# Column maxima over 128 partitions: from TensorE's transposes to a reduction on GpSimd

## The chip, the cores and the metric

The kernel runs on one core of one Trainium2 chip. A core has five engines with an instruction queue each: TensorE (PE in the profile; PEld is its weight load), VectorE (DVE), ScalarE (ACT), GpSimd (POOL) and SyncE (SP). All but SP compute on SBUF, a memory of 128 partitions; PE writes to PSUM, which DVE and ACT read and GpSimd does not. An engine works through its queue in order and waits on semaphores for the others. The metric is the device time of one execution in microseconds. Before the change it is 846.99 us, the median of three runs (846.04 to 847.17).

## The reference

Eight batches of linear attention, and one gated feed-forward layer over all their tokens:

```python
q_s = exp(q - max(q, axis=-1));  q_s = q_s / (sum(q_s, axis=-1) + 1e-9)
k_s = exp(k - max(k, axis=2));   k_s = k_s / (sum(k_s, axis=2) + 1e-9)   # axis 2: the sequence
kv  = einsum('bhsd,bhse->bhde', k_s, v)
x   = einsum('bhsd,bhde->bhse', q_s, kv)       # -> 4608 tokens x 512
h   = x @ w_in                                 # 512 -> 2048
out = (h * erf(softplus(h))) @ w_out           # 2048 -> 512
```

q, k and v have shape 8 x 8 heads x 576 x 64, all in float32. The maximum of k runs over the sequence. The sequence lies on the partitions, so this maximum goes across them: it needs the largest of 128 partitions for each of 512 columns (8 heads of 64), and then every partition needs the result.

## The kernel before

**Feed-forward.** The 4608 tokens are taken in 12 blocks of 384 (three to a pair of batches), and each block in four groups of 512 hidden columns: 48 steps n. In a step, `mm1` multiplies weights with x (banks pX, pY, pZ), `softplus` and `erf` run on ACT, `gmul`, `ghi` and `glo` (L1037, L1051, L1055) multiply and split the result into two float16 tiles on DVE, and `mm2` (L1083) adds three float16 products for each float32 one into banks o0 to o2. The products of `mm1` (L957) are a seven-product scheme, whose sums are made as the banks pX, pY, pZ are emptied: by DVE at L969, L971, L979 and L982, by ACT at L974, L976 and L984. Each of these three banks exists once, so the next product into it waits until it is empty. The first six steps are in float32 (`mm1_32`, L1074), while the weights are being decoded.

**Attention.** Batch 0 is written out at the start. `attention(b)` for batches 1 to 7 is a generator: it is traced in pieces between the steps of the feed-forward, `pace` taking pieces as fast as the shares in `SHARES` say. For each batch it does the following.

- `k_max` (L503 to L507, DVE): maxima of k within each partition, into `asc[:, 0]`, 128 x 512. `asc` is one tile with two halves of 512 columns; the second half is a scratch of the same function, and later other steps use both.
- `k_max_T` (L514, L518): four PE transposes put the 512 columns onto partitions, in a PSUM bank with the tag `bk`; DVE reduces them to `km`, 128 x 4.
- `q_sub` (L460, L461, DVE): the maxima of q along the row, and their subtraction.
- `k_max_rows` (L527): four PE transposes of the broadcast `km` put the maximum of each column onto all partitions, in the other `bk` bank, `kB`.
- L683, L688 (DVE): k and its tail less `kB`. Then the exponentials on ACT, the products k'v on PE (`kv_mm`, L548), and their normalisation (`kv_norm`, L567 to L571) into `asc[:, 0]`.
- `kv_max`, `kv_split`: DVE takes the largest magnitude of each partition (L584, `mx`, 128 x 1); `all_max` makes it one number for all partitions by a PE transpose of the broadcast column (L128) and a DVE reduction (L130, `e`); from it `scale_of_max` derives a power of two and its inverse (L131 to L144), and L601 and L602 split the scaled k'v into two float16 tiles `kvbd`.
- `x_mm` (L660): q times kvbd on PE; ACT writes the result into the block x (L449).

**What GpSimd does.** Constants and zero fills at the start, one subtraction for batch 0 (L826), some weight loads (L191), the zero fill of `kvbd` for batches 2 and 3 (L596), and for each batch two small fills of `vtail` (L439, L440) ahead of the load of v's last rows.

**What sets the order.** `ORDER` and the loops at the end give the program order by hand. A planner then makes each engine's queue from it when the program is built: program order is its priority, and its own estimate of durations tells it when an instruction is ready; an instruction that is ready early may run in a gap ahead of older ones. On ACT the feed-forward's functions and the exponentials are chained to program order (`act`). Semaphores and waits follow from the tiles.

## Time and profile before

| | |
|---|---|
| median of three runs | 846.99 us (846.04 to 847.17) |
| profiled execution: time, span | 847.39 us, 845.4 us |
| granted TensorE clock | 1.0 of full speed |
| PE busy | 817.5 us, 97% |
| DVE busy | 631.9 us, 75% |
| ACT busy | 506.6 us, 60% |
| POOL busy | 18.1 us, 2%, 37 instructions |
| kT transposes (L514), kB transposes (L527), the scale's (L128) | 32, 32 and 8 matmuls of 128x128 in float32 |

The profile is one execution; its times count from the first instruction. A line of the timeline is: start, length, engine, line, operation, tile written <- tiles read, shapes, count, and in brackets the idle time before it and what ended that. PE's matmuls overlap and their ends are modelled, so the cost of one in PE's stream is the distance to the next start, not its length.

### The profile page before, as it was taken

What the parts mean: (1) busy time and instruction counts of PE and PEld (TensorE: products, weight loads), DVE (VectorE), ACT (ScalarE), POOL (GpSimd) and SP (SyncE); (2) the same over time, 40 slices, a digit from 0 to 9 for tenths busy, and PEclk for the clock granted to TensorE, in tenths of its full rate; (3) what the DMA queues carried; (4) which work ended last, traced back from release to release, by engine and by line L of the source; (5) the groups of instructions that cost most, each with busy time, mean ns of one, the idle gap of its engine ahead of it and who ended that gap; (6) DMA issues with size and microseconds to landing.
All of it is one profiled execution on the core that took longest, in us unless ns stands there. A gap on an engine that the chain in (4) does not pass through costs nothing.

```text
span 845.4 us, 15123 instructions
## 1 busy us (share of the span) xinstructions
PE 817.5 (97%) x6336; PEld 554.3 (66%) x6336; DVE 631.9 (75%) x900; ACT 506.6 (60%) x638; POOL 18.1 (2%) x37
## 2 busy tenths in 40 slices
PE   3999999999999999999999999999999999999996
PEld 2655555666766766766776776766776776767662
DVE  6899689998998869867877769867876657553543
ACT  2597659876674567465665467465665475544532
POOL 2101100000000000000000000000000000000000
PEclk9999999999999999999999999999999999999999
DMA  9975920023226303411171203411131100100100
GB/s 267 403 189 168 210 52 38 1 58 75 63 51 127 88 19 76 106 38 27 46 151 30 76 19 76 106 39 26 40 74 13 40 1 1 39 1 2 38 1 38
DMA packets 141347, 61.53 MB, mean 73 GB/s; under 512 B 130528, under 2 KB 132576, under 8 KB 141280
## 3 DMA queue, kind: packets, MB, share of 16 engines
q1 hardware_dynamic: 139104, 52.18, 24.9%
q0 software_dynamic: 2176, 8.39, 2.9%
q8 instruction: 50, 0.82, 0.4%
q14 instruction: 17, 0.14, 0.1%
HBM read 45.09 MB, written 9.44 MB: 64 GB/s over the span
## 4 chain that ended last, share of the span: by engine, by line
PE 66%; DVE 16%; ACT 10%; DMA 3%; issue 3%; SPq 1%; POOL 0%; ACTq 0%; DVEq 0%; POOLq 0%
PE o L1083 28%; PE pX L957 15%; PE pZ L957 8%; PE o L1074 4%; ACT G L350 3%; PE pY L957 3%; ACT L350 3%; DVE G L1037 2%; PE kv L548 2%; DVE H L1055 2%; DMA q<-in_q_dram 1%; PE x L660 1%; SPq L415 1%; ACT wt L301 1%; DVE wt L302 1%
## 5 line engine op out<-in xcount | busy, mean ns | idle before, releaser
L1083 PE MATMUL o<-wt,H 128*128 128x512 f16 x1512 | 347.4, 379 | 1.8 <-DVE H L1051 1.3
L957 PEld LDWEIGHTS <-wt 128*128 128x128 f16 x3528 | 294.0, 98 | 29.3 <-issue 5.6
L1083 PEld LDWEIGHTS <-H 128*128 128x128 f16 x1512 | 145.9, 98 | 150.8 <-DVE H L1051 1.8
L957 PE MATMUL pX<-x,wt 128*128 128x192 f16 x2016 | 193.9, 246 | 1.8 <-ACT H L976 0.7
L350 ACT ACT_TABLE_LOAD x105 | 134.7, 1283 | 3.2 <-DVE H L982 1.2
L1037 DVE SCALAR_TENSOR_TENSOR G<-G,small,H 128x1536 f32<-128x1536 f32 x44 | 79.9, 1817 | 46.2 <-ACT G L350 45.9
L984 ACT COPY H<-pX 128x384 f32<-128x384 f32 x42 | 20.0, 477 | 136.8 <-PE pX L957 131.4
L957 PE MATMUL pZ<-x,wt 128*128 128x192 f16 x1008 | 98.2, 246 | 0.0
L350 ACT ACTIVATE G<-H,U 128x768 f32<-128x768 f32 (+1 forms) x56 | 69.3, 1255 | 22.1 <-DVE H L982 21.5
L1055 DVE TENSOR_TENSOR H<-G,H 128x1536 f16<-128x1536 f32 x42 | 73.8, 1756 | 1.0
L350 ACT ACTIVATE G<-G 128x1536 f32<-128x1536 f32 x48 | 71.3, 1486 | 0.5
L449 ACT ACTIVATE x<-x 128x384 f32<-128x384 f32 (+1 forms) x52 | 17.7, 388 | 59.4 <-PE x L660 56.9
L957 PE MATMUL pY<-x,wt 128*128 128x192 f16 x504 | 48.4, 246 | 0.0
L982 DVE TENSOR_TENSOR H<-pZ,H 128x384 f32<-128x384 f32 x42 | 23.2, 553 | 28.9 <-PE pZ L957 28.9
L301 ACT ACTIVATE x<-x 128x768 f16<-128x768 f32 (+1 forms) x44 | 32.9, 762 | 16.4 <-DVE x L394 16.3
L969 DVE COPY H<-pY 128x384 f32<-128x384 f32 x42 | 23.3, 554 | 25.8 <-PE pY L957 25.8
L1051 DVE CAST H<-G 128x1536 f16<-128x1536 f32 x42 | 40.2, 957 | 0.8
L302 DVE SCALAR_TENSOR_TENSOR x<-x,x 128x768 f16<-128x768 f32 (+1 forms) x44 | 37.4, 853 | 3.2 <-ACT x L301 3.2
L1099 DVE TENSOR_SCALAR ob<-o,V 128x512 f32<-128x512 f32 x29 | 21.7, 749 | 21.9 <-PE o L1083 21.8
L996 PE MATMUL pX<-x,wt 128*128 128x384 f32 x96 | 33.9, 488 | 0.0
L971 DVE TENSOR_TENSOR H<-pX,H 128x384 f32<-128x384 f32 x42 | 23.3, 555 | 13.3 <-PE pX L957 12.5
L460 DVE TENSOR_REDUCE q_m<-q 128x16 f32<-128x1024 f32 x14 | 17.1, 1219 | 17.9 <-DMA q<-in_q_dram 17.9
(182 smaller groups left out, 851.1 us busy)
## 6 DMA issues: line engine op xcount, KB each, us to landing
out_dram<-ob SPq DMA_DIRECT2D x32, 256.0 KB, 2.3
vbuf<-in_v_dram SPq DMA_DIRECT2D x60, 128.0 KB, 3.2
q<-in_q_dram SPq DMA_DIRECT2D x56, 128.0 KB, 3.3
k<-in_k_dram SPq DMA_DIRECT2D x56, 128.0 KB, 3.4
wt<-in_moe_w_out_dram POOLq DMA_DIRECT2D x5, 1024.0 KB, 8.7
wt<-in_moe_w_in_dram SPq DMA_DIRECT2D x4, 1024.0 KB, 10.6
wt<-in_moe_w_out_dram SPq DMA_DIRECT2D x2, 1024.0 KB, 15.6
H_raw<-in_k_dram SPq DMA_DIRECT2D x2, 512.0 KB, 5.0
```

Source lines behind the costliest of these rows:

```text
L301: nc.scalar.activation(hi, src, AF.Copy, scale=s)
L302: nc.vector.scalar_tensor_tensor(lo, src, s, hi, op0=ALU.mult, op1=ALU.subtract)
L350: i = nc.scalar.activation(out_, in_, func, **kw)
L957: nc.tensor.matmul(o, w[wl][:, c, a * P:(a + 1) * P], x[:, xl, xi, c, :], start=(new and a == 0 and c == 0 and i == 0), stop=(c == 1 and i ...
L969: nc.vector.tensor_copy(C[0, 0], bank2("Y"))
L971: add(C[0, 0], bank2("X"), C[0, 0], op=ALU.add)
L996: nc.tensor.matmul(ph[:, :T], w[:, c, a * P:(a + 1) * P], x[:, c, :], start=(c == 0), stop=(c == NC4 - 1),)
L1037: nc.vector.scalar_tensor_tensor(flat(s["G"]), flat(s["G"]), GA32 if n < N32 else GA[:, g:g + 1], flat(s["H"]), op0=ALU.mult, op1=ALU.mult,)
L1051: nc.vector.tensor_copy(flat(s["gh"]), flat(s["G"]))
L1055: nc.vector.tensor_tensor(flat(s["gl"]), flat(s["G"]), flat(s["gh"]), op=ALU.subtract)
L1074: nc.tensor.matmul(o, s["G"][:, a, ts_], w[:, a, :], start=(first_ and a == 0), stop=(last_ and a == FG - 1),)
L1083: nc.tensor.matmul(o, s[gt][:, a, ts_], w[wl][:, a, :], start=(first_ and a == 0 and i == 0), stop=(last_ and a == FG - 1 and i == 2),)
```

## The change

From batch 2 on, two reductions across partitions are one GpSimd instruction each, `partition_all_reduce`, which writes the largest value over 128 partitions to all of them. The first takes `asc[:, 0]` (128 x 512) and writes `asc[:, 1]`, which L683 and L688 then read in the place of the PSUM bank kB. The second takes `mx` (128 x 1) and writes `e`. Batches 0 and 1 keep the transposes, and so do the weights' scales.

```diff
-    def all_max(mx, name):
-
-        bk = psa.tile([P, 512], F32, tag="bk", name=f"{name}_bk")
-        nc.tensor.transpose(bk[:, :P], mx.to_broadcast([P, P]), ident)
+    def all_max(mx, name, pool):
+
         e = at.tile([P, 1], F32, tag="sc_e", name=f"{name}_e")
-        nc.vector.tensor_reduce(e, bk[:, :P], axis=AX.X, op=ALU.max)
+        if pool:
+            nc.gpsimd.partition_all_reduce(e, mx, P, RED.max)
+        else:
+            bk = psa.tile([P, 512], F32, tag="bk", name=f"{name}_bk")
+            nc.tensor.transpose(bk[:, :P], mx.to_broadcast([P, P]), ident)
+            nc.vector.tensor_reduce(e, bk[:, :P], axis=AX.X, op=ALU.max)
         nc.vector.tensor_scalar_max(e, e, TINY)
         return e
...
-    E32, QDMA = 2, 3
+    E32, QDMA, KPOOL = 2, 3, 2
...
-        s, u = scale_of_max(mx, f"x{b}")
+        s, u = scale_of_max(mx, f"x{b}", b >= KPOOL)
...
-        km = k_max_T(b, kmax)
+        if b < KPOOL:
+            km = k_max_T(b, kmax)
+        else:
+            kb = asc[:, 1].rearrange("p (h d) -> p h d", h=H)
+            nc.gpsimd.partition_all_reduce(asc[:, 1], asc[:, 0], P, RED.max)
         q_sub(rows(qs[0]), 16, f"q_{b}_0")
         yield SHARES[1]
-        kb = k_max_rows(b, km)
+        if b < KPOOL:
+            kb = k_max_rows(b, km)
```

## The prediction

> **What bounds the kernel now.** I read the page first: its own span, and who is busy in it.

> ```profile
> span 845.4 us, 15123 instructions
> ...
> PE 817.5 (97%) x6336; PEld 554.3 (66%) x6336; DVE 631.9 (75%) x900; ACT 506.6 (60%) x638; POOL 18.1 (2%) x37
> ```

> Matmul ends are modelled, so 97% alone proves little. I therefore took the busy time by stretches (columns: length, then PE, PEld, DVE, ACT and POOL busy with their counts, clock, DMA share, GB/s), and then the order of PE's own work.

> ```profile
> 150.00:200.00 50.00, 49.59 (x388) 33.31 (x386) 48.03 (x74) 40.41 (x44) 0.63 (x2) 1.00 0.20 46
> 200.00:250.00 50.00, 47.17 (x406) 33.56 (x405) 43.89 (x60) 30.95 (x41) 0.00 (x0) 1.00 0.19 47
> ...
> 350.00:800.00 450.00, 449.48 (x3839) 319.04 (x3838) 310.55 (x428) 256.45 (x302) 1.27 (x4) 1.00 0.18 42
> ```

> From 350 us to 800 us PE lacks 0.52 us in 450, at the full clock (1.00). The timeline shows that this is real work: groups follow one another at a fixed spacing, each starting where the one before ran out.

> ```profile
> 399.35 2.75 PE L1083 MATMUL o<-wt,H 128*128 128x512 f16 x12
> 401.94 0.60 PE L514 MATMUL kT<-ident,asc 128*128 128x128 f32 x4
> 402.38 1.15 PE L957 MATMUL pZ<-x,wt 128*128 128x192 f16 x12
> ...
> 406.34 2.75 PE L1083 MATMUL o<-wt,H 128*128 128x512 f16 x12
> 408.93 0.60 PE L527 MATMUL kB<-ident,km 128*128 128x128 f32 x4
> 409.36 1.15 PE L957 MATMUL pZ<-x,wt 128*128 128x192 f16 x12
> ...
> 439.28 2.75 PE L1083 MATMUL o<-wt,H 128*128 128x512 f16 x12
> 441.87 0.27 PE L128 MATMUL x_bk<-ident,mx 128*128 128x128 f32 x1
> 441.98 1.15 PE L957 MATMUL pZ<-x,wt 128*128 128x192 f16 x12
> ```

> Twelve L1083 matmuls take 2.59 us from start to start, both at 399.35 and at 406.34. So PE's stream is the bound in this stretch, and what leaves the stream is time. Before 350 us it is nearly so, but DVE is close behind: 48.03 of 50 us in the stretch from 150 us. There a late DVE instruction reaches PE at once.

> **Part 1, the transposes that leave PE.** By start-to-start spacing the four kT transposes cost 402.38 − 401.94 = 0.44 us, the four kB 409.36 − 408.93 = 0.43 us, and the scale's one 441.98 − 441.87 = 0.11 us: 0.98 us a batch. Six batches (2 to 7) have the change: 5.9 us.

> One transpose group also stops the stream. In batch 3 PE reaches kB before DVE has the column maxima (km):

> ```profile
> 237.68 0.33 PE L957 MATMUL pZ<-x,wt 128*128 128x192 f16 x2
> 239.22 0.65 PE L527 MATMUL kB<-ident,km 128*128 128x128 f32 x4 [1.21 <-DVE km L518]
> ```

> That wait of 1.21 us goes with kB. What is late next there is DVE's own work, which gets lighter too (below), so I count the 1.2 us in full.

> **Part 2, DVE.** Two groups of its instructions lose their six of eight, and one reads from elsewhere:

> ```profile
> L461 DVE TENSOR_TENSOR q<-q,q_m 128x1024 f32<-128x1024 f32 x14 | 17.1, 1220 | 0.2
> L683 DVE TENSOR_TENSOR k<-k,kB 128x1024 f32<-128x1024 f32 x14 | 16.7, 1216 | 0.3 <-PE kB L527 0.3
> ...
> L518 DVE TENSOR_REDUCE km<-kT 128x4 f32<-128x512 f32 x8 | 5.5, 690 | 7.2 <-PE kT L514 7.2
> ...
> L130 DVE TENSOR_REDUCE x_e<-x_bk 128x1 f32<-128x128 f32 x8 | 2.3, 289 | 5.8 <-PE x_bk L128 5.7
> ```

> DVE loses 0.69 + 0.29 = 0.98 us a batch, as much as PE. So the gain of part 1 also stands where DVE is the closer bound, before 350 us. The subtraction L683 now takes its maxima from SBUF (asc) and not from PSUM (kB). L461 is the same shape with both inputs in SBUF: 1220 against 1216 ns, nothing. No transfer and no ACT instruction is added or moved. Three uses a batch of the two `bk` banks disappear, which can only free them earlier.

> **Part 3, the reductions on GpSimd.** No such instruction is in the trace, so its duration is bounded by other rows of GpSimd:

> ```profile
> 0.24 0.10 POOL L1218 MEMSET const-float32-0.0<- 128x1 f32 x1 [0.24 <-issue]
> ...
> 16.27 1.91 POOL L826 TENSOR_TENSOR q<-G_raw,q_m 128x1024 f32<-128x1024 f32 x1 [12.35 <-DVE q_m L825]
> ...
> 96.17 0.72 POOL L191 DMA_DIRECT2D wt<-in_moe_w_out_dram  x1 [2.47 <-DVE x_s L143]
> ...
> 117.18 0.96 POOL L596 MEMSET kvbd<- 128x1024 f16 x1 [12.58 <-PE x L657]
> 187.09 0.53 POOL L439 MEMSET vtail<- 64x520 f32 x1 [68.94 <-issue]
> ```

> L826 takes 1.91 us for 1024 columns, so 512 columns take at least 0.95 us: the lower end. For the upper end I estimate no overlap at all: eight steps from one group of 16 partitions to the next, and 16 more inside a group, each at L826's rate, (8 + 16) × 0.95 = 22.9 us. I take the eight steps alone, 7.6 us, because a fold inside 16 partitions by halves is few steps and can run under the next columns. For the scale (one column) the ends are 0.10 us (the 128x1 memset) and 24 × 0.10 = 2.4 us; I take 8 × 0.10 = 0.8 us.

> GpSimd is free for it: after the memset at 117.18 it does nothing until 187.09, and its last weight load is issued at 96.17. The new instruction waits for L507 (the last step of the column maxima). Behind it on GpSimd stand only the vtail memsets for the following batch, which wait for a later product of the same batch anyway. If the first call has a preparation of its own, it falls into the same empty stretch. [...]

> What hides the 7.6 us is the distance between L507 and L683, the first reader of the result:

> ```profile
> 122.78 0.67 DVE L507 TENSOR_TENSOR asc<-asc,kt 64x512 f32<-64x512 f32 x1
> ...
> 174.05 1.22 DVE L683 TENSOR_TENSOR k<-k,kB 128x1024 f32<-128x1024 f32 x1
> ```

> ```profile
> 226.68 0.69 DVE L507 TENSOR_TENSOR asc<-asc,kt 64x512 f32<-64x512 f32 x1
> ...
> 239.91 2.35 DVE L683 TENSOR_TENSOR k<-k,kB 128x1024 f32<-128x1024 f32 x2 [0.28 <-PE kB L527]
> ```

> ```profile
> 361.93 0.69 DVE L507 TENSOR_TENSOR asc<-asc,kt 64x512 f32<-64x512 f32 x1
> 363.82 1.82 DVE L1037 SCALAR_TENSOR_TENSOR G<-G,small,H 128x1536 f32<-128x1536 f32 x1 [1.20 <-ACT G L350]
> 365.67 0.96 DVE L1051 CAST H<-G 128x1536 f16<-128x1536 f32 x1
> 366.67 1.76 DVE L1055 TENSOR_TENSOR H<-G,H 128x1536 f16<-128x1536 f32 x1
> 368.93 0.56 DVE L979 TENSOR_TENSOR H<-pX,H 128x384 f32<-128x384 f32 x1 [0.50 <-PE pX L957]
> ...
> 409.80 1.21 DVE L683 TENSOR_TENSOR k<-k,kB 128x1024 f32<-128x1024 f32 x1
> ```

> Batch 2 has 174.05 − 123.45 = 50.6 us, batch 3 12.5, batch 5 47.2. At 7.6 us all is covered. At 22.9 us batch 3 is not: 10.4 us stick out. For the scale, the path of before in its shortest batch is

> ```profile
> 261.27 0.41 DVE L584 TENSOR_REDUCE mx<-asc 128x1 f32<-128x256 f32 x1
> ...
> 263.96 0.29 DVE L130 TENSOR_REDUCE x_e<-x_bk 128x1 f32<-128x128 f32 x1 [1.21 <-PE x_bk L128]
> ```

> From mx (261.68) to the end of x_e (264.25) it takes 2.6 us, so anything up to 2.4 us is no later than today: cost nothing.

> **The sum.** 5.9 + 1.2 = 7.1 us less. Against the profiled execution: span 845.4 − 7.1 = 838.3 us, and the 2.0 us that lie around the span (its time is 847.39) give 840.3. The median of the runs, 846.99, is 0.4 below that execution: 839.9. **I forecast 840 us.** Other places of idle PE before 350 us, and another order of the same work, give the likeliest case its own range of 837 to 843.

> **The rivals.**

> *DVE is shut out while GpSimd reads (the other side).* GpSimd and DVE both read SBUF. In this kernel nothing shows how they share it. Beside L826 (16.27 to 18.18), the only long reading instruction of GpSimd, DVE ran these two, of which the first has kB from PSUM and the second one input:

> ```profile
> 16.05 1.20 DVE L814 TENSOR_TENSOR k<-H_raw,kB 128x1024 f32<-128x1024 f32 x1
> 17.18 1.21 DVE L467 TENSOR_REDUCE q_r<-q 128x16 f32<-128x1024 f32 x1
> ```

> If DVE cannot read two SBUF tiles while the reduction runs, the first victim in batch 5 is L1037 (G and H, both in SBUF). With 7.6 us the reduction runs from 362.6 to 370.2, so L1037 is 6.4 us late. Behind it in DVE's queue L1051, L1055 and L979 take 4.6 us from L1037's start to L1055's end (363.82 to 368.43): L979 would start at 374.8 and free pX at 375.4. PE needs pX for

> ```profile
> 372.24 1.15 PE L957 MATMUL pX<-x,wt 128*128 128x192 f16 x12
> ```

> and stands still for 3.2 us. In batches 2 to 4, where DVE has little to give, I charge the whole 6.4. Sum: 3 × 3.2 + 3 × 6.4 − 7.1 = +21.7, so 869. It decides from about 4 us on: there L979 frees pX at 371.8, in time, batches 2 to 4 pay 2.8 each, and 8.4 − 7.1 = +1.3 gives 848, no change. [...] Chance 0.32: 0.12 for the short reduction (no change), 0.20 for the long one.

> *DVE waits for the result.* The order on each engine is fixed when the program is built. Today L683 stands where it does because kB comes so late (in batch 3 it starts 0.28 us after waiting for kB). With PE out of the path L683 may be placed sooner behind L507 than the reduction needs. DVE then waits at the head of its queue, with L1037 and the evacuations behind it. Placed right behind the two q instructions (2 × 1.22), a reduction of 7.6 us is 5.2 us late; by the working above batches 5 to 7 pass on 2.0 of that (3.2, less the 1.2 by which 5.2 is shorter than 6.4), batches 2 to 4 all of it: 6.0 + 15.6 − 7.1 = +14.5, so 861. It decides from the point where the reduction is longer than the distance that is left. Against it: today's smallest distance is 12.5 us. Chance 0.16. [...]

> *Half the gain stays behind.* If before 350 us ACT and not PE or DVE ends the waits, batches 2 to 4 give nothing: 3 × 0.98 = 2.9 us, so 844. PE's 47.17 of 50 us from 200 us leaves room for that. Chance 0.05.

> *More than the sum.* With L683 free of PE it can run in DVE's idle time, and PE's missing 2.8 us in the stretch from 200 us may shrink too: 835 to 837. Chance 0.06.

> *It doesn't do what it says.* The switch is b < 2 in all three places, so there is no way for it to be without effect; no chance.

> **How the numbers follow.** Hidden as in the sum 0.41, more 0.06, half 0.05, shut out short 0.12 and long 0.20, late result 0.16. Faster: 0.41 + 0.06 + 0.05 = 0.52, of which I give 0.02 to no change. What a measurement of this kernel can tell from no change is 0.2%, 1.7 us. No change 0.12 + 0.02 = 0.14, slower 0.36. The range goes from 836.5 down at the better case to 862 at the late result; left out are a little of the first and most of the long lock-out, together about 0.2.

> **What would show it.** Right: no kT, kB or x_bk from batch 2 on, PE's sums of L514, L527 and L128 down to two batches, the all-reduce ending before L683 in every batch, and the length of 350 to 800 shorter by about 3 × 0.98. Wrong: DVE instructions with two SBUF inputs that become longer, or start late, exactly while the all-reduce runs; or "DVE k L683 <- POOL asc" among the waits. The reduction's own duration decides: under 4 us the forecast holds even with a shared port, above 12.5 us not even without one.

## The result, and the profile after

The changed kernel takes 864.71 us (median, 863.86 to 864.89); the kernel before took 847.17 us beside it. The ratio is 1.0212, with a 95% interval of 1.0201 to 1.0224: slower by 2.1%. The profiled execution took 863.86 us with a span of 862.0 us.

The page after, its span and busy times:

```profile
span 862.0 us, 15004 instructions
...
PE 815.8 (95%) x6282; PEld 551.1 (64%) x6282; DVE 631.1 (73%) x888; ACT 506.2 (59%) x638; POOL 31.3 (4%) x49
```

The edit is all there: PE has 54 matmuls fewer (6336 − 6282 = 6 batches × 9), DVE 12 instructions fewer, GpSimd 12 more. The groups of instructions show that the new ones are short (columns: count, then busy us and mean ns, then idle time before them and what ended it):

```profile
L693 DVE TENSOR_TENSOR k<-k,asc 128x1024 f32<-128x1024 f32 x12 | 14.6, 1220 | 6.2 <-POOL asc L687 6.2
...
L687 POOL PARTITION_ALL_REDUCE asc<-asc x6 | 10.8, 1801 | 81.2 <-DVE asc L512 60.8 <-ACT x L454 14.6 <-PE ws_in L270 5.9
...
L131 POOL PARTITION_ALL_REDUCE x_e<-mx x6 | 2.2, 362 | 105.4 <-DVE mx L589 105.4
```

(Lines below the import have moved: L507, L683, L979 and L957 of before are L512, L693, L989 and L967 here. k's all-reduce is L687, the scale's L131.) k's reduction over partitions takes 1.80 us, the scale's 0.36 us, and L693 costs as much from SBUF (1220 ns) as L683 of before did from PSUM (1216 ns). By the durations alone the change should have paid. The time was lost in two other places.

**The start.** The timeline of before, from its first instruction: the affine select that makes the identity for every transpose, and PE's first transposes (its line ends with the idle time before it and what ended that).

```profile
1.92 0.29 POOL masks.py:199 TENSOR_SCALAR_AFFINE_SELECT ident<-ident 128x128 f32<-128x128 f32 x1
...
9.04 1.08 PE L514 MATMUL kT<-ident,asc 128*128 128x128 f32 x4 [9.04 <-DVE asc L507]
```

The same stretch after:

```profile
12.62 0.28 POOL masks.py:199 TENSOR_SCALAR_AFFINE_SELECT ident<-ident 128x128 f32<-128x128 f32 x1 [10.74 <-issue]
...
12.95 1.12 PE L519 MATMUL kT<-ident,asc 128*128 128x128 f32 x4 [12.95 <-POOL ident masks.py:199]
```

**Batches 5 and 7.** The timeline after, where batch 5's maxima are ready (DVE, GpSimd, and the PE line that they hold up; the other lines are left out):

```profile
355.11 0.69 DVE L512 TENSOR_TENSOR asc<-asc,kt 64x512 f32<-64x512 f32 x1
355.83 0.75 DVE L1109 TENSOR_SCALAR ob<-o,V 128x512 f32<-128x512 f32 x1
355.89 1.79 POOL L687 PARTITION_ALL_REDUCE asc<-asc  x1 [6.06 <-DVE asc L512]
...
357.71 1.23 DVE L693 TENSOR_TENSOR k<-k,asc 128x1024 f32<-128x1024 f32 x1 [1.13 <-POOL asc L687]
358.85 1.81 DVE L1047 SCALAR_TENSOR_TENSOR G<-G,small,H 128x1536 f32<-128x1536 f32 x1
...
360.58 1.22 DVE L693 TENSOR_TENSOR k<-k,asc 128x1024 f32<-128x1024 f32 x1
361.72 0.95 DVE L1061 CAST H<-G 128x1536 f16<-128x1536 f32 x1
...
363.25 1.75 DVE L1065 TENSOR_TENSOR H<-G,H 128x1536 f16<-128x1536 f32 x1
364.91 0.55 DVE L989 TENSOR_TENSOR H<-pX,H 128x384 f32<-128x384 f32 x1
...
365.52 2.08 PE L967 MATMUL pX<-x,wt 128*128 128x192 f16 x12 [4.36 <-DVE H L989]
```

The subtraction L693 no longer stands 47 us behind the end of the column maxima but 1.9 us (355.80 to 357.71). It is DVE's next but one instruction after them: DVE waits 1.13 us for the all-reduce, then spends two subtractions on k, which nobody needs yet. L1047 stands behind the wait and the first subtraction, the rest of its chain (L1061, L1065, L989) behind the second as well. PE needs L989 to free pX and stops for 4.36 us. The twelve pX matmuls after the stop take 2.08 us, not 1.15 as before. The same happens at 554 us in batch 7 (there L693 starts at 554.38, again after a wait of 1.13 us, and PE stops for 4.36 us). The windows after:

```profile
350.00:400.00 50.00, 44.79 (x344) 31.15 (x343) 31.55 (x44) 20.29 (x30) 1.79 (x1) 0.97 0.14 38
550.00:600.00 50.00, 45.64 (x350) 31.94 (x349) 30.27 (x35) 20.53 (x30) 1.79 (x1) 0.97 0.14 38
350.00:800.00 450.00, 437.21 (x3700) 309.08 (x3699) 302.62 (x413) 249.70 (x295) 7.71 (x10) 0.99 0.17 42
```

Of the 12.8 us that PE now lacks between 350 and 800 us (0.5 before), 5.2 and 4.4 lie in these two stretches, and only there is the clock below 1.00 (the other seven stretches of 50 us have 1.00). In the waits the two steps stand by name (us in total, times, longest); the first line is from before, where L979 is the same evacuation:

```profile
PE pX L957 <- DVE H L979: 0.3, 1, 0.3
...
PE pX L967 <- DVE H L989: 10.1, 5, 4.4
DVE k L693 <- POOL asc L687: 6.2, 4, 2.0
DVE x_e L136 <- POOL x_e L131: 2.0, 3, 0.9
```

### The profile page after: what moved, and what is told of

It is laid out like the page before. It is cut to its first block, busy times and chain, and to the rows that moved or that the text cites. A ratio compares the mean times of both kernels' runs of the same rounds, so it can differ in the third digit from the quotient of the medians.

```text
span 862.0 us, 15004 instructions
## 1 busy us (share of the span) xinstructions
PE 815.8 (95%) x6282; PEld 551.1 (64%) x6282; DVE 631.1 (73%) x888; ACT 506.2 (59%) x638; POOL 31.3 (4%) x49
## 4 chain that ended last, share of the span: by engine, by line
PE 43%; DVE 7%; ACT 4%; issue 2%; DMA 1%; SPq 1%; POOL 0%; ACTq 0%; DVEq 0%; POOLq 0%
PE o L1093 21%; PE pX L967 12%; PE pZ L967 5%; PE pY L967 3%; ACT L355 1%; DVE G L1047 1%; PE x L665 1%; ACT G L355 1%; DVE H L1065 1%; DVE H L1061 1%; DVE x L307 1%; ACT q L355 1%; SPq L420 0%; PE kv L553 0%; DMA q<-in_q_dram 0%
## 5 line engine op out<-in xcount | busy, mean ns | idle before, releaser
L967 PEld LDWEIGHTS <-wt 128*128 128x128 f16 x3528 | 296.8, 98 | 52.1 <-issue 26.6
L967 PE MATMUL pX<-x,wt 128*128 128x192 f16 x2016 | 195.6, 247 | 19.9 <-DVE H L989 10.1
L1047 DVE SCALAR_TENSOR_TENSOR G<-G,small,H 128x1536 f32<-128x1536 f32 x44 | 79.9, 1816 | 64.0 <-ACT G L355 64.0
L967 PE MATMUL pZ<-x,wt 128*128 128x192 f16 x1008 | 97.2, 246 | 0.0
L1065 DVE TENSOR_TENSOR H<-G,H 128x1536 f16<-128x1536 f32 x42 | 73.8, 1756 | 1.0
L967 PE MATMUL pY<-x,wt 128*128 128x192 f16 x504 | 50.0, 250 | 0.0
L979 DVE COPY H<-pY 128x384 f32<-128x384 f32 x42 | 23.3, 554 | 27.1 <-PE pY L967 27.0
L1061 DVE CAST H<-G 128x1536 f16<-128x1536 f32 x42 | 40.2, 958 | 1.0
L307 DVE SCALAR_TENSOR_TENSOR x<-x,x 128x768 f16<-128x768 f32 (+1 forms) x44 | 37.9, 866 | 3.4 <-ACT x L306 3.2
L1109 DVE TENSOR_SCALAR ob<-o,V 128x512 f32<-128x512 f32 x29 | 21.7, 748 | 19.9 <-PE o L1093 19.9
L981 DVE TENSOR_TENSOR H<-pX,H 128x384 f32<-128x384 f32 x42 | 23.3, 555 | 13.4 <-PE pX L967 12.8
L465 DVE TENSOR_REDUCE q_m<-q 128x16 f32<-128x1024 f32 x14 | 17.1, 1220 | 17.8 <-DMA q<-in_q_dram 17.8
```

What stands on the lines that cost most here:

```text
L307: nc.vector.scalar_tensor_tensor(lo, src, s, hi, op0=ALU.mult, op1=ALU.subtract)
L967: nc.tensor.matmul(o, w[wl][:, c, a * P:(a + 1) * P], x[:, xl, xi, c, :], start=(new and a == 0 and c == 0 and i == 0), stop=(c == 1 and i ...
L979: nc.vector.tensor_copy(C[0, 0], bank2("Y"))
L981: add(C[0, 0], bank2("X"), C[0, 0], op=ALU.add)
L1047: nc.vector.scalar_tensor_tensor(flat(s["G"]), flat(s["G"]), GA32 if n < N32 else GA[:, g:g + 1], flat(s["H"]), op0=ALU.mult, op1=ALU.mult,)
L1061: nc.vector.tensor_copy(flat(s["gh"]), flat(s["G"]))
```

## The experiments

Theory: two things cost the time. The code that the all-reduce needs has to be exchanged again when the next execution starts (some 4 to 5 us); and L693, freed from kB, is placed too early in DVE's queue (most of the rest). Rivals: the loss at the start is a fixed cost of having the instruction in the program; or the reduction itself, by its own time and by what it holds up on DVE, costs what the place seems to cost.

**The old code back, at the end of the program.** Behind the last attention step a GpSimd addition of one column is issued, whose result nobody reads:

```diff
     assert next(att, 1) == 1
+    ux = bat[B - 1]["ux"]
+    nc.gpsimd.tensor_tensor(small[:, 40:41], ux, ux, op=ALU.add)
```

> The changed kernel (864.7 us) with one tiny GpSimd addition on one column behind the last all-reduce, so that the code that GpSimd held before the first all-reduce is loaded again at the end. Theory: the 4.3 us at the start come from a load of GpSimd code that the all-reduce of the execution before has pushed out (GpSimd stands still for 10.74 us ahead of the identity matrix, and PE's first transposes wait for it). Then the identity is written at about 1.9 us again, the first transposes start at 9.0 instead of 13.0, and the time is 864.7 - 4.3 = 860.4. Rival: the load comes with every start of a program that holds an all-reduce, whatever was left behind: 864.7, no change.

Measured: 859.39 us, ratio to before 1.0151 (1.0138 to 1.0165). From the timeline of this kernel:

```profile
2.15 0.29 POOL masks.py:199 TENSOR_SCALAR_AFFINE_SELECT ident<-ident 128x128 f32<-128x128 f32 x1 [0.29 <-POOL kvbd L115]
...
8.79 1.09 PE L519 MATMUL kT<-ident,asc 128*128 128x128 f32 x4 [8.79 <-DVE asc L512]
...
648.09 0.18 POOL L1215 TENSOR_TENSOR small<-x_u 128x1 f32<-128x1 f32 x1 [7.00 <-issue]
```

The 10.74 us at the start are gone, and PE starts at 8.79 again. The wait has gone along with the addition: it now stands idle for 7.00 us at 641 us, where GpSimd has nothing else to do. So the affine select waits long (10.74 us) when an all-reduce ran last on GpSimd in the program, and not (0.29 us) when the addition did; by the theory it pays for code that an earlier execution left behind. All kernels here agree: in the four with this addition the affine select starts at 2.15 us, in the four with an all-reduce and without the addition between 12.62 and 13.03. The start is worth 1.0212 − 1.0151 = 0.0061, 5.2 us, give or take 1.5 us by the two intervals.

**The subtraction held in its place.** Only the three subtractions of k and kt are kept in program order on DVE:

```diff
+        pin = tc.keep_in_program_order if b >= KPOOL else (lambda i: i)
         for hf in range(2):
-            nc.vector.tensor_tensor(
+            pin(nc.vector.tensor_tensor(
...
-            )
-        nc.vector.tensor_tensor(kt, kt, kb[tl], op=ALU.subtract)
+            ))
+        pin(nc.vector.tensor_tensor(kt, kt, kb[tl], op=ALU.subtract))
```

> The changed kernel with the three subtractions of k (L693, L698) from batch 2 on held behind every DVE instruction that stands before them in the program, so that DVE takes them as late as in the kernel before. The all-reduces stay. Theory: the two losses of 5.8 us (batches 5 and 7) come from the place of these subtractions in DVE's queue, some 50 us earlier than before, ahead of the multiplication and the evacuation that PE waits for. Then both go, and what was forecast comes through behind the start: 847.2 + 4.3 - 7.1 = 844.4, with 843 to 850 allowed. Rival: the loss comes from what the all-reduces themselves do to DVE (waits for the scale's result, the shared port): then at most the 6.2 us of waiting for the k all-reduce go, and the time stays above 857.

Measured: 846.88 us, ratio 1.0006 (0.9997 to 1.0015). In the timeline of this kernel, batch 5:

```profile
357.33 0.55 DVE L990 TENSOR_TENSOR H<-pX,H 128x384 f32<-128x384 f32 x1
...
358.69 1.79 POOL L687 PARTITION_ALL_REDUCE asc<-asc  x1 [13.49 <-DVE asc L512]
...
411.05 1.22 DVE L694 TENSOR_TENSOR k<-k,asc 128x1024 f32<-128x1024 f32 x1
```

The all-reduce ends at 360.48 and a subtraction of k stands at 411.05 again, behind many rounds of evacuation. The place in the queue is worth 1.0212 − 1.0006 = 0.0206, 17.4 us (give or take 1.2): much more than the two stops of batches 5 and 7, which the theory put at 5.8 us each. The time came out 2.5 us above the theory's 844.4, inside the 843 to 850 that it allowed.

The two traces show where the rest is. DVE copies pY (L979 in the changed kernel, L980 here) once in every step from the seventh on; I compare when the same step's copy starts. The changed kernel falls behind this one by 4.7 us in batches 2 to 4 (up to 344 us of before), by 5.0 us more around batch 5 (up to 423 us), 1.7 around batch 6, 5.0 around batch 7 and 0.4 behind it: 16.8 us in these two executions.

**Both edits together.**

> Both edits together. Theory: 844.4 - 4.3 = 840 us, the time that was forecast for the change, and faster than the kernel before by 0.8%. If only one of the two causes is right, 860 or 844; if the gain of 7.1 us on PE was miscounted, about 847.

Measured: 842.18 us (841.7 to 843.64), ratio 0.9952 (0.9938 to 0.9965). This kernel is faster than both. It keeps 4.1 us of the predicted 7.1. Its timeline in batch 3 shows one reason:

```profile
236.24 1.81 DVE L307 SCALAR_TENSOR_TENSOR x<-x,x 128x768 f16<-128x768 f32 x2
237.97 0.55 DVE L990 TENSOR_TENSOR H<-pX,H 128x384 f32<-128x384 f32 x1
...
238.57 1.15 PE L968 MATMUL pX<-x,wt 128*128 128x192 f16 x12 [1.27 <-DVE H L990]
```

Before, PE stood still for 1.21 us just here, for kB. Now there is no kB, and PE stands still for 1.27 us for pX's evacuation: DVE was the late engine both times, and kB had only been where the lateness arrived. DVE is rid of the reduction L518 (0.69 us) here, but the all-reduce makes another of its instructions longer in this batch (by 0.59 us in the changed kernel, 1.14 against 0.55, see below), and DVE has no idle time between the two.

A second reason: PE also stops for L990 in batch 5 (0.99 us, at 352.62) and in batch 7 (0.78 us, at 542.74), where before had no such stop. From the copy of pY at 344 us on this kernel gains only 1.4 us on before; by part 1 of the prediction it would be 3 × 0.98 = 2.9.

**Without k's all-reduce.** The early place stays, the reduction goes:

```diff
-            kb = asc[:, 1].rearrange("p (h d) -> p h d", h=H)
-            nc.gpsimd.partition_all_reduce(asc[:, 1], asc[:, 0], P, RED.max)
+            kb = kmax
```

> The changed kernel without the all-reduce for k: from batch 2 on the subtractions read the maxima of their own partition (the reduction over partitions is left out, so k is scaled by another factor in each partition). DVE can then take the subtractions at once and never waits for GpSimd for them; the scale's all-reduce and the code load at the start stay. Theory (the place of the subtractions is the cause): still slow, 860 to 868, with PE stalls of 4 to 5 us in batches 5 and 7. Rival (DVE's waits for the k all-reduce and the port that it holds are the cause): they are gone, so about 864.7 - 11.6 = 853.

Measured: 858.71 us, ratio 1.0140 (1.0125 to 1.0155). Batch 5 of this kernel:

```profile
356.30 1.22 DVE L692 TENSOR_TENSOR k<-k,asc 128x1024 f32<-128x1024 f32 x1
...
360.63 0.55 DVE L988 TENSOR_TENSOR H<-pX,H 128x384 f32<-128x384 f32 x1
361.23 2.08 PE L966 MATMUL pX<-x,wt 128*128 128x192 f16 x12 [3.13 <-DVE H L988]
```

With no reduction to wait for, PE still stops for 3.13 us of the 4.36, and for 3.14 in batch 7. So of the place's 17.4 us, 1.0212 − 1.0140 = 0.0072, 6.1 us, go with the all-reduce, and 11.3 us are the early place alone (both give or take 1.6). The rival's 853 is refuted. The theory was also too high: 858.71 lies below its 860 to 868, and the stops are shorter than its 4 to 5 us. The start still pays here (the affine select starts at 12.94 us, after 11.07 us idle): the scale's all-reduce alone is enough for that.

The 6.1 us are near the 6.2 us that DVE waits for the all-reduce in the list of waits above, but the two need not be the same: DVE's waits in batches 5 and 7 are 1.13 us each, and PE's stop in batch 7 is here followed by matmuls at full speed, which it is not in the changed kernel.

**Only the scale on GpSimd.** k's maxima go through the transposes as before:

```diff
-        if b < KPOOL:
-            km = k_max_T(b, kmax)
-        else:
-            kb = asc[:, 1].rearrange("p (h d) -> p h d", h=H)
-            nc.gpsimd.partition_all_reduce(asc[:, 1], asc[:, 0], P, RED.max)
+        km = k_max_T(b, kmax)
...
-        if b < KPOOL:
-            kb = k_max_rows(b, km)
+        kb = k_max_rows(b, km)
```

> Only the scale is taken on GpSimd from batch 2 on; k's maxima are transposed by TensorE as before, and nothing is added at the end. Theory (any GpSimd reduction over partitions brings the code load, and the next execution pays for it at its start; k's subtraction at the head of DVE's queue costs the rest): about +4.3 us at the start, 6 x 0.11 = 0.7 us less on PE, at most 1 us of waits for x_e, so 849 to 852; the identity's affine select ends near 13 us and PE's first kT starts near 13. Rival (only k's large reduction brings the load, or the reductions cost time where they run): the affine select near 2 us, and 845 to 847.

Measured: 849.63 us, ratio 1.0041 (1.0025 to 1.0056). The timeline of this kernel:

```profile
12.94 0.28 POOL masks.py:199 TENSOR_SCALAR_AFFINE_SELECT ident<-ident 128x128 f32<-128x128 f32 x1 [11.07 <-issue]
...
197.07 1.28 DVE L307 SCALAR_TENSOR_TENSOR wt<-wt,small,wt 128x1024 f16<-128x1024 f32 x1 [0.28 <-ACT wt L306]
197.23 1.36 POOL L131 PARTITION_ALL_REDUCE x_e<-mx  x1 [6.11 <-DVE wt L307]
```

The start pays for the small reduction (11.07 us idle) as for the large one (10.74), and that is about all that this part alone costs.

**The reduction beside, with nobody waiting.** k and the scale use the transposes; k's all-reduce runs as well, and its result is not read. The addition at the end is in:

```diff
-        if b < KPOOL:
-            km = k_max_T(b, kmax)
-        else:
-            kb = asc[:, 1].rearrange("p (h d) -> p h d", h=H)
+        km = k_max_T(b, kmax)
+        if b >= KPOOL:
             nc.gpsimd.partition_all_reduce(asc[:, 1], asc[:, 0], P, RED.max)
...
-        if b < KPOOL:
-            kb = k_max_rows(b, km)
+        kb = k_max_rows(b, km)
...
-        s, u = scale_of_max(mx, f"x{b}", b >= KPOOL)
+        s, u = scale_of_max(mx, f"x{b}", False)
```

> The transposes stay and are used for k and for the scale, as before; k's all-reduce runs beside them into a tile that nobody reads, and the tiny GpSimd addition at the end brings the old code back before the next execution. [...] Theory (the reduction itself is nearly free; waiting for it is what costs): 846 to 848.5. Rival (the reduction holds DVE up by itself, which would be the 6 to 7 us that were still unaccounted for without it): 851 to 854.

Measured: 846.40 us against 845.67 us before it, ratio 1.0010 (1.0001 to 1.0018). The groups of this kernel:

```profile
L690 DVE TENSOR_TENSOR k<-k,kB 128x1024 f32<-128x1024 f32 x14 | 16.6, 1212 | 0.3 <-PE kB L532 0.3
...
L685 POOL PARTITION_ALL_REDUCE asc<-asc x6 | 11.0, 1832 | 130.5 <-DVE asc L512 108.7 <-PE x L665 21.8
```

Six reductions of 1.83 us run, and the kernel pays 0.7 us for all of them (0.1 to 1.5 by the interval). The trace shows where: in batch 3 the reduction makes one DVE instruction, L307, 0.6 us longer (1.15 us, 0.55 in before), DVE has no idle time behind it, and PE's stop for kB is 0.59 us longer than the 1.21 us of before:

```profile
239.49 0.65 PE L532 MATMUL kB<-ident,km 128*128 128x128 f32 x4 [1.80 <-DVE km L523]
```

So neither the instruction (1.83 us) nor its hold-up of DVE (0.6 us) is the cost, in this order of the work. For most of the 6.1 us that went with the all-reduce that leaves DVE's waiting for it at the head of the queue; this is argued from what is left, and no run shows it by itself.

**Both edits, with the scale on TensorE again.** As the fastest kernel, with `scale_of_max(mx, f"x{b}", False)`.

> Both edits of the fastest kernel (old code back at the end, the three subtractions kept in program order), but the scale is taken by TensorE's transposes again. Theory (scale's part is worth its 0.11 us a batch on PE and costs nothing): 842.2 + 0.7 = 842.9 (842 to 844). Rival (DVE waits longer for the scale from GpSimd than for the transposed one, so that this part costs): 840 to 841.8.

Measured: 841.51 us, ratio 0.9948 (0.9935 to 0.9960). The rival's number came out, but the comparison's kernel before was 0.56 us faster than in the first one, and as ratios 0.9948 and 0.9952 can't be told apart. What the scale's part is worth stays open by the times. The traces lean to the rival's side, by another mechanism. With the scale on TensorE, PE has no stop for L990 in batches 5 and 7, and from the copy of pY at 344 us on it gains 2.3 us on before; with the scale on GpSimd it had the stops of 0.99 and 0.78 us and gained 1.4 (one execution each). DVE's waits for the all-reduce are short (0.46 us at 339.93 in the kernel with both edits). But the scale comes sooner there, and the steps that use it (L606, L607, from 342.38) stand ahead of the multiplication L1048 (346.76) and no longer behind it: the same kind of displacement as k's.

## Why the prediction was wrong

The forecast was 840 us, its range 836.5 to 862; the time is 864.71. Its steps:

- **Part 1, 5.9 us off PE: the nine matmuls a batch are gone, and most of their time is won.** The fastest kernel has 4.1 us of it left over everything.
- **Part 1, the 1.2 us of batch 3: wrong.** I counted the kB stall in full because DVE's work "gets lighter too". The kernel with both edits stops for 1.27 us in that place for L990. The wait named kB, but the late engine was DVE, and in that batch it got lighter by 0.69 us and heavier by 0.59.
- **Part 2: L693 from SBUF costs nothing more** (1220 ns against 1216). Right.
- **Part 3, the durations: mis-sized, on the safe side.** I took 7.6 us and 0.8 us; they are 1.80 and 0.36. The eight and sixteen steps behind my figures were an assumption; no run shows such steps. By the prediction's own last sentence ("under 4 us the forecast holds even with a shared port") the forecast should have held. That sentence was wrong, since duration was not what decided. It also contradicts the prediction's own working, which has 848 us for about 4 us with DVE shut out.
- **Part 3, the preparation: half right.** I let it "fall into the same empty stretch" of GpSimd. The wait ahead of the first all-reduce does: from 123.01 us (MODIFY_POOL_CONFIG) to

```profile
128.71 1.86 POOL L687 PARTITION_ALL_REDUCE asc<-asc  x1 [5.89 <-PE ws_in L270]
```

  it is 5.7 us, with nobody waiting. In four of the other kernels GpSimd's idle time ahead of its first reduction is 5.69 to 6.11 us (5.89 in this row). What I left out, and so put at nothing, is the way back: ahead of the affine select of the next execution, at a moment when PE waits for the identity, GpSimd stood idle for 10.74 us, and it cost 5.2 us by the first experiment. That both waits are loads of code is my theory.
- **Part 3, the cover: the step that failed.** "What hides the 7.6 us is the distance between L507 and L683" took the 12.5 to 50.6 us of before as given. They were made by kB's long way through PE. The change removed that way, and the program's builder moved L693 up from 47.2 us behind L507 to 1.9 us in batch 5. I had this as the rival "DVE waits for the result", at 0.16, with the condition that the reduction be longer than the distance left, and 861 us. Its place and its victims are right (L1037's successors, pX, PE). Its price was wrong: it charged only the wait for the reduction, and even without any reduction 11.3 us of the 17.4 remain, where the subtractions themselves stand ahead of the evacuations. That its 861 lies near the 864.71 is luck. By its working a reduction of 1.80 us, placed behind two q instructions of 1.22, would never have been late.
- **The rival "DVE is shut out": a hold-up is there, and small.** I gave it 0.32 and up to 869 us. That GpSimd and DVE share a port was an assumption, which no run shows; the rows show how long instructions took. In batch 3 after:

```profile
230.35 1.79 POOL L687 PARTITION_ALL_REDUCE asc<-asc  x1 [34.32 <-DVE asc L512]
...
230.66 1.14 DVE L307 SCALAR_TENSOR_TENSOR x<-x,x 128x384 f16<-128x384 f32 x1
```

  The same instruction, where no reduction runs:

```profile
123.64 0.55 DVE L307 SCALAR_TENSOR_TENSOR x<-x,x 128x384 f16<-128x384 f32 x1
```

  With its two SBUF inputs it is 0.59 us longer inside the reduction. But it ends at 231.80, 0.34 us before the reduction does. In the kernel with the reduction beside, a multiplication with two SBUF inputs that starts 1.04 us into a reduction takes its usual 1.82 us:

```profile
363.38 1.78 POOL L685 PARTITION_ALL_REDUCE asc<-asc  x1 [21.80 <-PE x L665]
...
364.42 1.82 DVE L1044 SCALAR_TENSOR_TENSOR G<-G,small,H 128x1536 f32<-128x1536 f32 x1 [1.21 <-ACT G L355]
```

  By these rows (GpSimd's spans are rough) the reduction of batch 3 held up this DVE instruction until about 0.9 us after its own start (0.31 + 0.59), and not for its whole length, as the rival had it. In batch 2 two small instructions that start late in a reduction (L277, 0.57 and 0.47 us; 0.15 and 0.17 before) do end with it. Beside the reductions of batches 4 to 7 no DVE instruction of the changed kernel is longer than elsewhere.

The sum over the whole change, in ratios: −4.1 us that both edits leave, 5.2 at the start, 17.4 from the place: 18.5, against a measured 0.0212 × 847.17 = 18.0. The two causes add up within the intervals, and nothing of size is left unexplained. Of the place's 17.4, some 10 us fall around batches 5 and 7 by the comparison of the copies of pY. How the rest divides into single stalls was not taken apart.

## What to carry to other kernels

Work that gets its input sooner moves in a queue whose order the builder chooses: look at what it moves ahead of, and hold it in its place if nobody needs it early. The distance between a producer and its reader is part of what a change alters, so it is no cover for the change's own latency. A GpSimd instruction of a new kind brought two waits here, ahead of its own first run (5.7 us, hidden) and ahead of the next execution's affine select (10.74 us idle, 5.2 us of the time); a small instruction of the old kind, issued late where GpSimd is idle, moved the second wait out of the way (7.00 us there).

## What the runs showed that I had not expected

What the program runs last on GpSimd shows at the program's start: GpSimd idles ahead of the same affine select for 0.29 us where that is the addition, and for 10.74 to 11.15 us where it is an all-reduce. Inside the program it waited 5.7 us at 123 us, ahead of the first all-reduce, and 7.00 us at 641 us, ahead of the addition. By the theory these are loads of code, and GpSimd's code outlives the execution.

The hold-up showed both ways, and in these rows the later one to start took longer. In batch 3 that was DVE (1.14 us against 0.55); in the kernel with only the scale on GpSimd the small reduction, 0.35 us where no such instruction runs, took 1.36 us and ended at 198.59, just behind L307, which had started 0.16 us before it and ended at 198.35. Twice more in that kernel it started 0.25 us behind an L307 and took 0.91 us. That the first to start shuts the other out for its whole length is not what the rows of k's reduction show (0.9 us of 1.8).

After PE had stood still for 4.36 us in batch 5, or for 3.13 us in the kernel without k's all-reduce, its next twelve matmuls took 2.08 us where they take 1.15, and the granted clock of that stretch of 50 us read 0.97; after 1.27 us they took 1.15. So each of these two stops cost PE at least 0.93 us more than its length.

But nearly the same stop, 3.14 us in batch 7 of that kernel, was followed by matmuls of full speed, and the clock of its 50 us read 1.00:

```profile
556.72 1.15 PE L966 MATMUL pX<-x,wt 128*128 128x192 f16 x12 [3.14 <-DVE H L988]
```

The traces' records of the granted clock show a difference. In the changed kernel the changes lie on a grid of 3.41 us: the clock is 0.50 from 364.80 to 368.21 and from 562.77 to 566.18, 58 × 3.413 later. Each of these two falls follows a grid period in which PE stood idle for most of the time, 3.41 and 2.82 us. In the kernel without k's all-reduce PE had been idle for 2.53 us ahead of the fall at 360.63 (its rows fit: the matmuls into pY at 363.10 take 1.62 us and not 1.15, and the next ones at 364.55 take 1.15 again). The stop of 3.14 us fell across two periods of that grid, 1.61 us in one and 1.53 in the other, and the clock stayed at 1.00. That the division into periods makes the difference is an inference from these four stops.
